# Order-of-work settings held for two first-pass steps instead of sixteen in a two-layer attention and GeGLU kernel

## The chip, the cores and the metric

The kernel runs on one core of one Trainium2 chip, in one launch. The metric is the device time of an execution in microseconds, as the median of several runs. TensorE (PE) does the matmuls and loads their weights (PEld), VectorE (DVE) and ScalarE (ACT) read its results out of the PSUM banks, GpSimd (POOL) works on SBUF alone, and SyncE (SP) issues the transfers.

## The reference

```python
def _A_ref(x, wqkv, wo):                 # S=2048, D=512, H=32 heads of Dh=16
    qkv = (x @ wqkv) ...                 # split into q, k, v by head
    scores = jnp.einsum("bhqd,bhkd->bhqk", q, k) * (Dh ** -0.5)
    p = _softmax(scores, axis=-1)
    o = jnp.einsum("bhqk,bhkd->bhqd", p, v)
    return o_reshaped @ wo
def _B_ref(x, w_gate, w_up, w_down):     # F=1792
    return (_gelu(x @ w_gate) * (x @ w_up)) @ w_down

x = A_x                                  # bfloat16, (1, 2048, 512)
x = x + _A_ref(_layernorm(x), A_wqkv, A_wo)
x = x + _B_ref(_layernorm(x), B_w_gate, B_w_up, B_w_down)
x = x + _A_ref(_layernorm(x), A_wqkv, A_wo)
x = x + _B_ref(_layernorm(x), B_w_gate, B_w_up, B_w_down)
```

Two layers with the same weights: attention over 2,048 tokens with 32 heads of 16 channels each, then a gated feed-forward part.

## The kernel before

All of `x`, the weights, K and V stay in SBUF. Queries are taken in blocks of 512 tokens (256 for the last two of the second layer, of which the last is split further at its end), and heads in 8 groups of four. One block and one group make a *unit*. A head has only 16 channels, so its scores use a 32-row strip of the PE array, and the four heads of a group lie on four strips.

**First pass.** For each unit, each 128 queries, each 512 keys and each head, one strip matmul (`p1_emit`, L1671) puts 128 x 512 scores into a PSUM bank, and DVE takes the maximum of each row, over one bank or two banks at once (L1686). A full unit has 64 such banks. `pos["p1"]` counts them in halves: two banks are one *first-pass step*, and the whole program has 2,048 steps. The maxima go through a few small POOL operations (L1027 to L1032) and a transfer (L1056) into an extra row of the queries, so that the second pass subtracts them inside its matmul. For some heads the maximum over two key blocks is *folded*: a matmul with the difference of the two blocks (`f_emit`, L1495), a relu on ACT (L1502) and a combined add and maximum on DVE (L1681).

**Second pass.** Strip matmuls with keys as rows (`p2_emit`, L1550) fill a bank with transposed scores, ACT takes the exponential of one bank or two (L1522), and `pv_emit` (L1575) multiplies them with V and a column of ones, using the whole array, into bank 7. When a unit is done, ACT copies bank 7 out (L1080) and POOL divides by the sum (L1086, L1091).

**The rest** runs in between as *chains* (Python generators that say what they wait for): projections and GEMMs in pieces (L782), their copies out of PSUM on ACT or DVE (L797, L799), the gate and the product of the feed-forward part (L1156 to L1238), layer norms, output projection, transfers. Each chain has a due time in first-pass steps.

**What sets the order.** Nothing is ordered by hand. While the program is being built, a loop (L1711 to L1864) keeps a clock for each engine, with a fixed length for each kind of instruction, and decides again and again what PE issues next: a bank for the first pass, one or two for the second, both, a piece of a chain, or a PV group. The other engines' instructions are put in behind the matmul that they read. Each engine then runs its own list in that order, with semaphores between the lists. Where the planner sees PE loaded below 0.55 (`WARM`) over its last 3.413 us, it adds a *filler* (`warm_emit`, L1704), a matmul of 240 columns whose result nobody reads.

The loop's decisions depend on 19 settings, and these are the subject here:

```python
STRETCH = 16
...
if pos["p1"] >= STRETCH * stretch[0]:
    if stretch[0] < len(PLAN):
        SPC, SPLIT, S1C, S2C, OV, LIM, NT, P2B, LAG, LAGT, FL, GL, FX, AHD, DUE, DUEM, PIECE, GP, NPV = PLAN[stretch[0]]
    stretch[0] += 1
```

`S1C` and `S2C` say how long before DVE or ACT runs dry its next bank is wanted, `SPC` and `SPLIT` how much may be lost by issuing both passes together, `OV` and `LIM` how far other work may run past that moment, `NT` and `P2B` how many and which banks the second pass may take at a time, `LAG`, `LAGT`, `FL`, `GL` and `FX` from which lead of the first pass on banks, copies and folding are given to the one or the other side, `AHD`, `DUE` and `DUEM` how far ahead due work is looked at, `PIECE` and `GP` in how many matmuls a GEMM is cut, and `NPV` when fillers are held to a higher load near the end of a unit. `PLAN` has 129 rows, one for each 16 steps.

Of the kernel before, what the change touches and what calls it, by code (L numbers as in the profile page):

```python
# [18 lines left out]
STRETCH = 16  # L20
PLAN = [
# [269 lines left out]
_T_MM = 1.0 / 2400.0  # L291
# [19 lines left out]
def _build(nc, x_in, wqkv, wo, wg, wu, wd, out, layer_blocks=((512, 512, 512, 512), (512, 512, 512, 256, 256)),  # L311
# [16 lines left out]
    with es:  # L328
# [62 lines left out]
        mode = ["full"]  # L391
        since = [0]
        T_DMA = 0.63
        act = []
        tw = {}
        tr = {}
        SEM = 0.06
# [1537 lines left out]
```

## Time and profile before

| | |
|---|---|
| time, median of 3 runs | 2483.9 us (2483.87 to 2483.9) |
| span of the profiled execution | 2482.0 us (no time of its own is given beside it; the median lies 1.9 us above) |
| instructions | 69,365 |
| PE busy | 2412.7 us, 97% |
| DVE busy | 2411.0 us, 97% |
| ACT busy | 2346.2 us, 95% |
| POOL busy | 1323.6 us, 53% |
| mean granted TensorE clock | 1.000 |

An engine counts as busy from an instruction's start to its end; the records of neighbours can overlap, so a busy engine may still have short gaps between starts. PE's busy time includes the fillers. In a group of instructions the first number is their busy time, the second the mean length of one in ns, the third the idle time of the engine just before them, followed by what ended most of it. "issue" stands for time in which the engine waited for nothing that the profile shows.

### The profile page before, as it was taken

The numbers are of one execution on the slowest core, as the hardware profiler recorded it, in microseconds if no ns is written. First come the engines' busy times: TensorE is split into PE (matmuls) and PEld (weight loads), VectorE is DVE, ScalarE is ACT, GpSimd is POOL, SyncE is SP. The second block draws the span as 40 slices with busy tenths as digits, with TensorE's granted clock in tenths as the row PEclk, the third lists the DMA queues.
The fourth block names the chain that finished last, engine by engine and source line by source line (L and its number), as shares of the span: only waits on it lengthen the run. The fifth ranks groups of instructions, "written<-read, shape, count | busy, mean of one in ns | idle before, by whom it ended". The sixth has DMA issues, their size and how long they took to land.

```text
span 2482.0 us, 69365 instructions
## 1 busy us (share of the span) xinstructions
PE 2412.7 (97%) x29824; PEld 1148.1 (46%) x29824; DVE 2411.0 (97%) x3167; ACT 2346.2 (95%) x3230; POOL 1323.6 (53%) x2182
## 2 busy tenths in 40 slices
PE   8999999999999999999999999999999999999999
PEld 3444444444444444444433555554444444544456
DVE  9999999999999999999999999999999999999995
ACT  7999999999999999999976999999999999999897
POOL 5121148965779367957143211379517882379472
PEclk9999999999999999999999999999999999999999
DMA  3110000000000000000000000000000000000000
GB/s 96 46 57 6 6 4 6 2 4 4 4 4 2 4 4 4 4 6 6 11 11 14 5 4 4 4 4 2 6 8 7 2 2 11 5 4 2 12 5 10
DMA packets 27387, 25.12 MB, mean 10 GB/s; under 512 B 9544, under 2 KB 26056, under 8 KB 27080
## 3 DMA queue, kind: packets, MB, share of 16 engines
q1 hardware_dynamic: 27080, 20.69, 2.9%
q8 instruction: 233, 3.82, 0.6%
q14 instruction: 74, 0.61, 0.1%
HBM read 9.70 MB, written 2.10 MB: 5 GB/s over the span
## 4 chain that ended last, share of the span: by engine, by line
PE 40%; DVE 37%; ACT 21%; issue 1%; POOL 1%; POOLq 0%; ACTq 0%; DVEq 0%
DVE PM L1686 35%; ACT SCR L1522 19%; PE PS L1671 13%; PE PS L782 10%; PE PS L1575 9%; PE PS L1550 4%; PE PS L1704 3%; DVE SCR L1681 1%; ACT SCR L1162 0%; ACT SCR L1502 0%; DVE HT L585 0%; PE PS L1495 0%; ACT AO L1236 0%; PE PS L904 0%; ACT XNT L799 0%
## 5 line engine op out<-in xcount | busy, mean ns | idle before, releaser
L1686 DVE TENSOR_REDUCE PM<-PS 128x1 f32<-128x512 f32 (+1 forms) x2586 | 2241.0, 932 | 33.1 <-PE PS L1550 11.6
L1522 ACT ACTIVATE SCR<-PS 128x1024 bf16<-128x1024 f32 (+1 forms) x2507 | 2029.0, 899 | 61.5 <-PE PS L1550 40.1
L1671 PE MATMUL PS<-KT,QT 32*128 32x512 bf16 x3940 | 1037.1, 384 | 38.6 <-DVE PM L1686 23.3
L1550 PE MATMUL PS<-QT,KT 32*128 32x512 bf16 (+2 forms) x4864 | 954.7, 349 | 6.8 <-ACT SCR L1522 5.2
L1575 PE MATMUL PS<-VP,SCR 128*128 128x51 bf16 (+1 forms) x16384 | 817.5, 187 | 12.0 <-ACT SCR L1522 6.9
L1575 PEld LDWEIGHTS PS<-VP,SCR 128*128 128x128 bf16 x16384 | 575.2, 96 | 509.0 <-issue 428.9
L1671 PEld LDWEIGHTS PS<-KT,QT 32*128 32x128 bf16 x3940 | 247.6, 91 | 515.7 <-DVE PM L1686 314.7
L1086 POOL TENSOR_TENSOR RL<-ACCS,CM 128x16 f32<-128x16 f32 (+2 forms) x66 | 179.6, 2722 | 384.8 <-ACT ACCS L1080 384.6
L1704 PE MATMUL PS<-WV,ZER 128*128 128x240 bf16 x1924 | 361.9, 265 | 1.2 <-ACT SCR L1522 1.1
L1550 PEld LDWEIGHTS PS<-QT,KT 32*128 32x128 bf16 x4864 | 241.6, 91 | 70.9 <-ACT SCR L1522 41.3
L1027 POOL TENSOR_TENSOR PM<-PM 128x32 f32<-128x32 f32 (+2 forms) x76 | 18.5, 243 | 305.1 <-DVE PM L1686 292.8
L1704 PEld LDWEIGHTS PS<-WV,ZER 128*128 128x128 bf16 x1924 | 147.9, 96 | 49.5 <-issue 39.6
L1238 POOL TENSOR_TENSOR HT<-HT,AO 128x512 bf16<-128x512 bf16 (+1 forms) x109 | 121.3, 1115 | 81.4 <-ACT AO L1236 80.4
L782 PE MATMUL PS<-XNT,WU 128*128 128x512 bf16 (+2 forms) x560 | 138.9, 339 | 1.2 <-ACT AO L1236 1.0
L782 PE MATMUL PS<-XNT,WG 128*128 128x512 bf16 (+2 forms) x560 | 139.7, 338 | 0.2 <-DVE XNT L797 0.2
L782 PE MATMUL PS<-WD,HT 128*128 128x512 bf16 x448 | 135.8, 381 | 0.2
L1275 POOL TENSOR_TENSOR KD<-KT 128x512 bf16<-128x512 bf16 x74 | 85.4, 1154 | 76.1 <-PE PS L1495 71.5
L1156 POOL TENSOR_TENSOR SCR<-HT 128x512 bf16<-128x512 bf16 (+1 forms) x98 | 96.0, 980 | 30.3 <-ACT HT L799 15.0
L1166 POOL TENSOR_TENSOR HT<-HT,SCR 128x512 bf16<-128x512 bf16 (+1 forms) x98 | 106.2, 1085 | 4.2
L1160 POOL TENSOR_TENSOR SCR<-SCR,HT 128x512 bf16<-128x512 bf16 (+1 forms) x98 | 106.3, 1086 | 1.8
L1681 DVE CUSTOM_DVE_ANT_0 SCR<-PS,SCR 128x512 bf16<-128x512 f32 x156 | 100.2, 686 | 1.9 <-PE PS L1495 0.6
L1106 POOL TENSOR_TENSOR X<-X,AO 128x512 f32<-128x512 f32 x42 | 53.2, 1268 | 84.4 <-ACT AO L1104 83.9
(129 smaller groups left out, 1560.4 us busy)
## 6 DMA issues: line engine op xcount, KB each, us to landing
KT<-SG SPq DMA_DIRECT2D x64, 64.0 KB
QT<-SG SPq DMA_DIRECT2D x56, 64.0 KB
QT<-MT SPq DMA_DIRECT2D x216, 1.0 KB
out_dram<-AO SPq DMA_DIRECT2D x16, 128.0 KB, 1.7
WG<-in_B_w_gate_dram SPq DMA_DIRECT2D x4, 448.0 KB, 4.3
WU<-in_B_w_up_dram SPq DMA_DIRECT2D x4, 448.0 KB, 4.8
WD<-in_B_w_down_dram SPq DMA_DIRECT2D x4, 384.0 KB, 4.5
QT<-MT SPq DMA_DIRECT2D x72, 0.5 KB
```

Source lines behind the costliest of these rows:

```text
L782: ins = e.matmul(out_ap, lhsT=l, rhs=r_, start=(i == 0), stop=(i == n - 1))
L1086: emit("pool", lambda e: e.tensor_tensor(RL[:, s, 0:4 * nq], lsum, CM1[:, 0:4 * nq], op=ALU.pow), r=[("ACCS", s), ("CM1",)], w=[("RL", s)] ...
L1160: emit("pool", lambda e: e.tensor_tensor(u, u, ht, op=ALU.mult), r=[ku, kh], w=[ku], dur=0.18 + n / 520.0)
L1166: emit("pool", lambda e: e.tensor_tensor(ht, ht, u, op=ALU.mult), r=[ku, kh], w=[kh], dur=0.18 + n / 520.0)
L1238: emit("pool", lambda e, ft=ft, o=o: e.tensor_tensor(HV[:, ft, :], HV[:, ft, :], AO[:, o, 0:n], op=ALU.mult), r=[("AO", o)] + ht_keys(ft, ...
L1522: emit("act", lambda e: e.activation(dst, src, ACTF.Exp, scale=DH ** -0.5), r=[BK[bk + i] for i in range(cnt)], w=[("PT", i) for i in slot ...
L1550: ins = e.matmul(bank(bk)[:, i * n:(i + 1) * n], lhsT=KT[32 * j:32 * j + 32, g, kt * 128:(kt + 1) * 128], rhs=QT[32 * j:32 * j + 32, s, c0 ...
L1575: ins = e.matmul(acc, lhsT=PT[:, slot, i * nh + (qt - q0) * 128:i * nh + (qt - q0 + 1) * 128], rhs=AP(VP, (kt * H + 4 * g + j) * 17, [[NTT ...
L1671: ins = e.matmul(bank(b), lhsT=QT[32 * j:32 * j + 32, s, qt * 128:(qt + 1) * 128], rhs=KT[32 * j:32 * j + 32, g, kb * 512:(kb + 1) * 512], ...
L1681: emit("dve", lambda e, i=i, b=b, sl=sl: e.tensor_tensor_reduce(PT[:, sl, :], bank(b), PT[:, sl, :], 1.0, -3.0e38, ALU.add, ALU.max, po[:, ...
L1686: emit("dve", lambda e: e.tensor_reduce(po, PS[:, bs[0]:bs[0] + cnt, :], axis=AX.X, op=ALU.max), r=bks, w=[("PM", sm) + h[1:] for h in hs] ...
L1704: return e.matmul(PS[:, b, NACC:512], lhsT=ZER[:, :], rhs=WV[:, 0, 0:512 - NACC], start=(b != 7), stop=(b != 7), skip_group_check=True)
```

## The change

`STRETCH` becomes 2, and `PLAN` becomes a dictionary: the settings that hold from step 2k on stand under the key k, and where a key is missing the last ones stay. It has 416 entries with 272 different sets of settings, among them all 104 different sets of before. Taken step by step, 657 of 1,025 pairs of steps have the settings that they had before. The list from which the planner reckons PE's load is kept as a queue with a running sum, which gives the same load. No function that emits an instruction is changed, and no buffer, size or bank count.

```diff
+import collections
...
-STRETCH = 16
-PLAN = [
-    (0.1, 0.15, 0.45, 0.42, 0.3, -0.05, 1, 1, 62, 84, 8, 60, 0.0, 2.0, 0, 2, 2, 2, 7),
-    (0.1, 0.15, 0.45, 0.42, 0.3, -0.05, 1, 1, 62, 84, 8, 60, 0.0, 2.0, 0, 2, 2, 2, 7),
-    (0.3, 0.3, 0.45, 0.42, 0.2, -0.05, 1, 1, 62, 84, 8, 20, 0.3, 1.5, 0, -14, 2, 2, 7),
...
+STRETCH = 2
+PLAN = {
+    0: (0.1, 0.15, 0.45, 0.42, 0.3, -0.05, 3, 1, 62, 84, 8, 60, 0.0, 2.0, 0, 2, 2, 2, 7),
+    2: (0.15, 0.5, 0.55, 0.42, 0.1, -0.05, 1, 2, 30, 124, 8, 100, 0.1, 2.0, 20, 6, 1, 2, 11),
+    6: (0.1, 0.0, 0.45, 0.62, 0.3, -0.05, 1, 1, 62, 84, 8, 60, 0.7, 2.0, 0, 2, 2, 2, 7),
+    7: (0.1, 0.15, 0.45, 0.42, 0.3, -0.05, 1, 1, 62, 84, 8, 60, 0.0, 2.0, 0, 2, 2, 2, 7),
...
-        act = []
+        act = collections.deque()
+        act_sum = [0.0]
+
+        def act_add(t, used):
+            act.append((t, used))
+            act_sum[0] += used
+
...
-                act.append((start, busy, n * (used or cols) * _T_MM))
+                act_add(start, n * (used or cols) * _T_MM)
...
-                    act.append((t, n * cols * _T_MM, n * cols * _T_MM / 4))
+                    act_add(t, n * cols * _T_MM / 4)
...
-                if stretch[0] < len(PLAN):
+                if stretch[0] in PLAN:
...
             while act and act[0][0] < now - 3.413:
-                act.pop(0)
-            load = sum(c for _, _, c in act) / 3.413
+                act_sum[0] -= act.popleft()[1]
+            load = act_sum[0] / 3.413
```

More of the change, by code (lines that the diff above doesn't have):

```diff
@@ L17 @@
 GELU_B = 0.044715
-STRETCH = 16
-PLAN = [
[129 rows of a table removed]
-]
+STRETCH = 2
+PLAN = {
[416 rows of a table added]
+}
 class _Op:
```

538 rows, old and new, of the table PLAN are left out of this document.

## The prediction

> **What bounds the kernel now.** I read the page first: the busy shares, the line of the granted clock, and the chain that ended last.
>
> ```profile
> span 2482.0 us, 69365 instructions
> PE 2412.7 (97%) x29824; PEld 1148.1 (46%) x29824; DVE 2411.0 (97%) x3167; ACT 2346.2 (95%) x3230; POOL 1323.6 (53%) x2182
> PEclk9999999999999999999999999999999999999999
> PE 40%; DVE 37%; ACT 21%; issue 1%; POOL 1%; POOLq 0%; ACTq 0%; DVEq 0%
> DVE PM L1686 35%; ACT SCR L1522 19%; PE PS L1671 13%; PE PS L782 10%; PE PS L1575 9%; PE PS L1550 4%; PE PS L1704 3%; DVE SCR L1681 1%; ACT SCR L1162 0%; ACT SCR L1502 0%; DVE HT L585 0%; PE PS L1495 0%; ACT AO L1236 0%; PE PS L904 0%; ACT XNT L799 0%
> ```
>
> Three engines are filled at once, and the chain goes from one to the other: row maxima on DVE (L1686), exponentials on ACT (L1522), matmuls on PE that feed both. There is no single wait to remove. What an order of work can change is the time between instructions. The same groups with their shapes kept apart give the prices, and the idle time before each:
>
> ```profile
> L1522 ACT ACTIVATE SCR<-PS 128x1024 bf16<-128x1024 f32 x1589 | 1560.3, 1065 | 48.8 <-PE PS L1550 32.5 <-PE PS L1671 0.2
> L1686 DVE TENSOR_REDUCE PM<-PS 128x2 f32<-128x1024 f32 x1198 | 1452.4, 1220 | 21.3 <-PE PS L1671 6.3 <-PE PS L1550 6.0
> L1686 DVE TENSOR_REDUCE PM<-PS 128x1 f32<-128x512 f32 x1388 | 932.2, 683 | 11.9 <-PE PS L1550 5.5 <-PE PS L1671 1.5
> L1522 ACT ACTIVATE SCR<-PS 128x512 bf16<-128x512 f32 x918 | 549.2, 613 | 12.6 <-PE PS L1550 7.7
> L1681 DVE CUSTOM_DVE_ANT_0 SCR<-PS,SCR 128x512 bf16<-128x512 f32 x156 | 100.2, 686 | 1.9 <-PE PS L1495 0.6 <-PE PS L1671 0.4 <-PE PS L1550 0.2
> L1502 ACT ACTIVATE SCR<-PS 128x1024 bf16<-128x1024 f32 x75 | 78.7, 1050 | 10.5 <-PE PS L1495 10.4
> L799 ACT ACTIVATE HT<-PS 128x512 bf16<-128x512 f32 x71 | 44.0, 620 | 0.0
> L1681 DVE DVE_READ_ACCUMULATOR2_ANT PM<- 128x1 f32 x156 | 13.1, 84 | 0.0
> L797 DVE CAST HT<-PS 128x512 bf16<-128x512 f32 x13 | 8.9, 682 | 0.1
> ```
>
> DVE stands still for 33.2 us (21.3 + 11.9) before all 2,586 row maxima together, ACT for 61.4 us (48.8 + 12.6) before all 2,507 exponentials. To see where, I asked for the busy time in forty stretches of 62 us:
>
> ```profile
> core 0: us, PE busy (x) PEld busy (x) DVE busy (x) ACT busy (x) POOL busy (x), PEclk, DMA share, GB/s
> 868.00:930.00 62.00, 60.07 (x760) 28.00 (x759) 61.96 (x71) 59.22 (x82) 39.94 (x87) 1.00 0.02 4
> 1302.00:1364.00 62.00, 60.44 (x464) 23.54 (x461) 57.82 (x105) 37.59 (x49) 19.23 (x51) 1.00 0.06 14
> 1488.00:1550.00 62.00, 60.14 (x869) 31.80 (x867) 61.19 (x74) 62.00 (x71) 10.82 (x12) 1.00 0.02 4
> 2418.00:2480.00 62.00, 60.02 (x950) 40.85 (x948) 33.48 (x74) 45.88 (x86) 18.93 (x43) 1.00 0.03 8
> ```
>
> Three kinds of stretch: DVE full (868 to 930, 61.96 of 62), ACT full (1488 to 1550, 62.00), and the end, where 28.5 us of DVE's 71.0 us of idle time (2482.0 less 2411.0) lie. At the turn between the layers (1302 to 1364) ACT is the one that starves. In the full stretches there is next to nothing visible to take. But the records of neighbouring instructions overlap, so "full" hides a little:
>
> ```profile
> 1411.59 29.45 ACT L1522 ACTIVATE SCR<-PS 128x1024 bf16<-128x1024 f32 x32
> ```
>
> Thirty-two exponentials in 29.45 us are 0.920 us each, where one record lasts 1.065 us. An exponential that starts 0.1 us late therefore still looks busy. The slack is somewhat more than the idle columns say, and still a few per cent at most.
>
> **What the change moves.** No source line of an instruction changes; what changes is the order that the planner writes, and with it the way in which some banks are evicted. I counted both built programs, instruction by instruction. Nothing on SP changes in number, so no transfer is added. On POOL there is one more two-column memset of PM, on an engine 53% busy. The last 1,449 PE instructions stand in the same order in both programs, and they hold the last 87 first-pass matmuls; after the last of these the four compute streams are the same too. So the 28.5 us at the end stay. Of PE's 29,824 instructions some 3,900 stand elsewhere, spread over nearly every stretch of the program in between; it is a small reshuffle.
>
> DVE: 6 one-bank maxima fewer (6 x 0.683 = 4.1 us), 1 two-bank maximum more (1.2 us), 2 folded maxima more with their reads (2 x (0.686 + 0.084) = 1.5 us), 1 copy of a gate tile fewer (0.7 us): 2.0 us less. ACT: 20 one-bank exponentials more (20 x 0.613 = 12.3 us), 10 two-bank ones fewer (10 x 1.065 = 10.7 us), 1 two-bank relu more (1.05 us), 1 gate copy more (0.6 us): 3.3 us more. So the work is as good as unchanged, and what counts is the waiting.
>
> The best sign of that is a count. The planner puts a filler matmul (L1704, output never used) where PE would else be less than 0.55 loaded (WARM) by its own reckoning. Two rows price it:
>
> ```profile
> L1704 PE MATMUL PS<-WV,ZER 128*128 128x240 bf16 x1924 | 361.9, 265 | 1.2 <-ACT SCR L1522 1.1
> 1345.68 0.89 PE L1704 MATMUL PS<-WV,ZER 128*128 128x240 bf16 x7
> ```
>
> Seven fillers in a row take 0.89 us, the last of them 0.265, so each other one occupies (0.89 - 0.265) / 6 = 0.104 us; the code counts 240 columns at 1/2400 us, 0.1 us. The changed program has 1,876 fillers, 48 fewer, and all other matmuls are the same in number. That is 4.8 us of PE time. Where fillers run, the load is held near 0.55, so a stretch with a given amount of real work needs fewer of them only if it is shorter, or if its real work lies more evenly. If it is all the former, the order is tighter by 4.8 / 0.55 = 8.7 us. If it is all the latter, by nothing. I take 8.7, because the counts fall in stretches that fillers fill as well as in others; zero stays in the range. The 2.0 us of DVE work are part of it and not added again.
>
> Two things are given back. The first is PE's change from strip matmuls (L1671, L1550, L1495) to full-array ones, which the table of waits prices:
>
> ```profile
> PEld PS L1575 <- issue: 428.9, 1875, 0.4
> PEld PS L1671 <- DVE PM L1686: 314.7, 1001, 1.6
> PEld PS L782 <- issue: 105.3, 462, 0.4
> ACT SCR L1522 <- PE PS L1550: 40.1, 119, 3.9
> PEld PS L1704 <- issue: 39.6, 174, 0.4
> DVE PM L1686 <- PE PS L1550: 11.6, 40, 0.8
> ```
>
> 428.9 / 1,875 = 0.229 us each, and L782 and L1704 have the same price (0.228). The changed order has 22 more such changes into L1575, 9 fewer into L782 and 10 fewer into L1704: 3 more, 0.7 us. The second is ACT's 3.3 us, of which 21%, ACT's share of the chain, is taken as lying on the path: 0.7 us. The rest is covered by ACT's own 135.8 us of idle time (2482.0 less 2346.2); in stretches like 1488 to 1550 that cover does not exist, and the whole 3.3 us would count.
>
> Sum: -8.7 + 0.7 + 0.7 = -7.3 us. On the profiled span that is 2482.0 - 7.3 = 2474.7 us; the median of the runs lies 1.9 us above that span (2483.9), and the runs agree within 0.03 us, so the forecast is 2476.6 us. What is late next is DVE itself: 314.7 us of weight loads wait for a maximum to free its bank, and a tighter order only lets PE wait longer there.
>
> One rule of the skill speaks against fewer fillers. The profile has a granted clock of 1.00 in each of the four stretches above and full marks in all forty slices, with fillers 1.3 us apart on average (2482.0 / 1,924). The Trainium skill, "TensorE: Matmul & The Clock Gate", Part 1, says that a matmul engine left idle for a window of about 3.4 us is set back to half its clock. By that rule 48 fillers fewer are harmless unless they leave a hole of that length; no run here shows a hole.
>
> **The rivals.** First, *the settings fit the planner's clock and not the chip* (0.20). The planner reckons with one fixed length for each kind of instruction and with no scatter. L1671 and L1550 take turns at the same banks, and the waits of DVE and ACT on L1550 are short and many (40 of 0.29 us, 119 of 0.34 us): these are what an order tuned to 0.1 us must hit. If the saved 8.7 us come back as some 30 such waits (30 x 0.3 = 9 us), nothing is left: 2484, give or take 5. For it speaks that only one instruction in eight moves; against it, that the tight row of ACT shows a plan carried out without gaps for 29 us.
>
> Second, *slower: the new changes of PE's mode lie where DVE is the bound* (0.14). The 22 further changes into L1575 cost 22 x 0.229 = 5.0 us if each delays a maximum, while the 19 saved ones lie before GEMMs and fillers that nobody waits for; with ACT's 3.3 us in full it makes +8.3 and up to 2492.2, less whatever part of the 8.7 is real. It decides once DVE's idle time before L1686 grows by more than 5 us from 33.2, with L1575 up in PE's waits. Against it: PE's 97% contains fillers, so it can give way.
>
> Third, *the clock falls* (0.04). If a stretch with load 0.55 is granted less than 0.55 of the clock, PE becomes its bound; at 0.5 a 62 us slice takes 0.55 / 0.5 = 1.1 times as long, +6.2 us, and one such slice gives 2490. That is the rule of the page named above, carried through. Nothing in the trace points to it.
>
> Fourth, *more gain than the fillers tell* (0.10). In stretches without fillers the count is blind. If half of the idle time of DVE before its maxima goes (16.6 us), it is 2467.
>
> That the change does nothing at all is excluded by the counts; that it does nothing to the time is the first rival.
>
> **How the numbers follow.** The forecast has 0.52, its own range 2472 to 2481. A measurement of this kernel can tell about 0.2%, 5 us, from no change: the borders are 2478.9 and 2488.9. Of the forecast's chance 0.08 lies above 2478.9. Faster: 0.44 + 0.10 = 0.54. Same: 0.08 + 0.20 = 0.28. Slower: 0.14 + 0.04 = 0.18. The range 2466 to 2490 leaves out about half of the fourth rival below and most of the second and third above, some 0.2.
>
> **What would show it.** Right: DVE's and ACT's busy times within 4 us of 2411 and 2346, filler busy time down by 2 to 3%, the last 62 us unchanged, and the saving spread in pieces of 0.1 to 0.5 us per stretch of 62 us, as less idle time before L1686 and L1522 or as closer starts behind the same busy share. Wrong: idle time before L1686 above 38 us; a granted clock under 1.00; or a saving that sits in one place, such as the turn of the layers.

## The result and the profile after

The changed kernel takes 2473.9 us (median of 5 runs, 2473.87 to 2474.03), the kernel before 2483.9 us (2483.87 to 2483.9): 10.0 us less, a ratio of 0.9959 with a 95% interval of 0.9947 to 0.9971. The forecast was 2476.6 us with a range of 2466 to 2490.

In the profile after, all line numbers are 294 higher (L1686 is L1980, L1522 is L1816, L1550 is L1844, L1575 is L1869, L1704 is L1998), except around the planner's load. First the span, the busy times and the chain that ended last:

```profile
span 2472.2 us, 69280 instructions
PE 2407.5 (97%) x29776; PEld 1147.3 (46%) x29776; DVE 2404.8 (97%) x3165; ACT 2343.1 (95%) x3242; POOL 1320.7 (53%) x2183
PEclk9999999999999999999999999999999999999999
PE 39%; DVE 38%; ACT 22%; issue 1%; POOL 1%; POOLq 0%; DVEq 0%; ACTq 0%
```

The picture is the same as before, 9.8 us shorter: DVE's busy time is down by 6.2 us and its idle time by 3.6 (71.0 to 67.4). No engine's share of the chain moves by more than one point. The groups with their shapes kept apart (busy us, mean ns of one, idle us before):

```profile
L1816 ACT ACTIVATE SCR<-PS 128x1024 bf16<-128x1024 f32 x1579 | 1550.3, 1071 | 41.4 <-PE PS L1844 27.9 <-PE PS L1965 0.4
L1980 DVE TENSOR_REDUCE PM<-PS 128x2 f32<-128x1024 f32 x1199 | 1451.2, 1217 | 21.3 <-PE PS L1844 6.4 <-PE PS L1965 6.4 <-PE PS L1789 0.3
L1980 DVE TENSOR_REDUCE PM<-PS 128x1 f32<-128x512 f32 x1382 | 925.2, 681 | 9.0 <-PE PS L1844 3.4 <-PE PS L1965 2.1
L1816 ACT ACTIVATE SCR<-PS 128x512 bf16<-128x512 f32 x938 | 559.8, 613 | 12.8 <-PE PS L1844 8.9
L1998 PE MATMUL PS<-WV,ZER 128*128 128x240 bf16 x1876 | 353.7, 265 | 0.8 <-ACT SCR L1816 0.7
```

The idle time before the maxima went from 33.2 to 30.3 us, before the exponentials from 61.4 to 54.2. The table of waits names the same waits, each a little shorter than before but the first, the weight loads of L1575 (L1869 here), which wait 3.2 us more:

```profile
PEld PS L1869 <- issue: 432.1, 1888, 0.4
PEld PS L1965 <- DVE PM L1980: 302.3, 977, 1.1
PEld PS L1076 <- issue: 104.4, 459, 0.4
PEld PS L1998 <- issue: 37.5, 163, 0.4
ACT SCR L1816 <- PE PS L1844: 36.8, 112, 3.9
DVE PM L1980 <- PE PS L1844: 9.8, 37, 0.7
```

And the end is untouched. The last 52 us of the kernel before, then the last 52 us after (busy time by engine: PE, PEld, DVE, ACT, POOL):

```profile
2430.00:2482.00 52.00, 48.79 (x743) 33.77 (x742) 21.70 (x58) 33.92 (x69) 8.99 (x20) 1.00 0.04 12
```

```profile
2420.20:2472.20 52.00, 48.73 (x743) 33.71 (x741) 21.63 (x58) 33.84 (x69) 8.90 (x20) 1.00 0.04 12
```

### The profile page after: what moved, and what is told of

Read it like the earlier page. It is cut to its first block, busy times and chain, and to the rows that moved or that the text cites. A ratio compares the mean times of both kernels' runs of the same rounds, so it can differ in the third digit from the quotient of the medians.

```text
span 2472.2 us, 69280 instructions
## 1 busy us (share of the span) xinstructions
PE 2407.5 (97%) x29776; PEld 1147.3 (46%) x29776; DVE 2404.8 (97%) x3165; ACT 2343.1 (95%) x3242; POOL 1320.7 (53%) x2183
## 4 chain that ended last, share of the span: by engine, by line
PE 39%; DVE 38%; ACT 22%; issue 1%; POOL 1%; POOLq 0%; DVEq 0%; ACTq 0%
DVE PM L1980 36%; ACT SCR L1816 20%; PE PS L1965 13%; PE PS L1076 10%; PE PS L1869 9%; PE PS L1844 4%; PE PS L1998 3%; DVE SCR L1975 1%; DVE HT L879 0%; ACT SCR L1456 0%; PE PS L1789 0%; ACT SCR L1796 0%; ACT AO L1530 0%; PE PS L1198 0%; ACT ACCS L1374 0%
## 5 line engine op out<-in xcount | busy, mean ns | idle before, releaser
L1980 DVE TENSOR_REDUCE PM<-PS 128x1 f32<-128x512 f32 (+1 forms) x2581 | 2234.2, 930 | 30.3 <-PE PS L1844 9.8
L1816 ACT ACTIVATE SCR<-PS 128x1024 bf16<-128x1024 f32 (+1 forms) x2517 | 2028.6, 900 | 54.3 <-PE PS L1844 36.8
L1844 PE MATMUL PS<-QT,KT 32*128 32x512 bf16 (+2 forms) x4864 | 951.7, 349 | 6.3 <-ACT SCR L1816 4.6
L1869 PE MATMUL PS<-VP,SCR 128*128 128x51 bf16 (+1 forms) x16384 | 818.6, 187 | 11.6 <-ACT SCR L1816 6.9
L1869 PEld LDWEIGHTS PS<-VP,SCR 128*128 128x128 bf16 x16384 | 576.5, 96 | 510.4 <-issue 432.1
L1965 PEld LDWEIGHTS PS<-KT,QT 32*128 32x128 bf16 x3938 | 247.5, 91 | 505.4 <-DVE PM L1980 302.3
L1998 PE MATMUL PS<-WV,ZER 128*128 128x240 bf16 x1876 | 353.7, 265 | 0.8 <-ACT SCR L1816 0.7
L1844 PEld LDWEIGHTS PS<-QT,KT 32*128 32x128 bf16 x4864 | 241.2, 91 | 72.4 <-ACT SCR L1816 44.1
L1998 PEld LDWEIGHTS PS<-WV,ZER 128*128 128x128 bf16 x1876 | 143.4, 96 | 46.5 <-issue 37.5
L1450 POOL TENSOR_TENSOR SCR<-HT 128x512 bf16<-128x512 bf16 (+1 forms) x98 | 95.9, 979 | 29.9 <-ACT HT L1093 14.7
```

The source lines that it names most:

```text
L1816: emit("act", lambda e: e.activation(dst, src, ACTF.Exp, scale=DH ** -0.5), r=[BK[bk + i] for i in range(cnt)], w=[("PT", i) for i in slot ...
L1844: ins = e.matmul(bank(bk)[:, i * n:(i + 1) * n], lhsT=KT[32 * j:32 * j + 32, g, kt * 128:(kt + 1) * 128], rhs=QT[32 * j:32 * j + 32, s, c0 ...
L1869: ins = e.matmul(acc, lhsT=PT[:, slot, i * nh + (qt - q0) * 128:i * nh + (qt - q0 + 1) * 128], rhs=AP(VP, (kt * H + 4 * g + j) * 17, [[NTT ...
L1965: ins = e.matmul(bank(b), lhsT=QT[32 * j:32 * j + 32, s, qt * 128:(qt + 1) * 128], rhs=KT[32 * j:32 * j + 32, g, kb * 512:(kb + 1) * 512], ...
L1980: emit("dve", lambda e: e.tensor_reduce(po, PS[:, bs[0]:bs[0] + cnt, :], axis=AX.X, op=ALU.max), r=bks, w=[("PM", sm) + h[1:] for h in hs] ...
L1998: return e.matmul(PS[:, b, NACC:512], lhsT=ZER[:, :], rhs=WV[:, 0, 0:512 - NACC], start=(b != 7), stop=(b != 7), skip_group_check=True)
```

## Experiments: where the gain sits, and what the settings are

Four theories were put to the test. **O**: the order is tighter throughout, and the fewer fillers are the shadow of that. **F**: the PE time of the fillers itself is the gain. **P**: the gain sits in one place. **D**: it is DVE's 2.0 us of work less.

**One layer at a time.** The first kernel takes the new settings for the first layer's 1,024 steps and the old ones after it, the second the other way round.

```diff
# e1: new settings for keys under 512, the old ones from there on; e2: the reverse
-PLAN = {all 416 entries}
+PLAN = {the new entries of one layer, the old rows of the other, each under its key}
```

> New settings for the first layer's 1,024 steps, old ones for the second; 25 fillers fewer than the kernel before, no other matmul more or less. Theory O (a tighter order throughout, which the filler count shadows at 0.1/0.55 = 0.18 us each): 4.5 us less than before, 2479.4. Rival P (the saving sits in one layer, or at its turn or end): nothing (2483.9) or all of it (2473.9).

> Old settings for the first layer, new ones for the second; 22 fillers fewer than before, no exponentials in more one-bank pieces. Theory O: 4.0 us less, 2479.9, so that both halves make up the whole. Rival P: all or nothing. Rival D (the saving is DVE's 2.0 us of work less): DVE has 6 one-bank maxima and one copy fewer and 3 two-bank maxima more here, 4.8 less 3.7 = 1.1 us, so 2482.8.

Measured: 2479.0 and 2479.0 us (ratios 0.9979 to the kernel before, 0.997 to 0.9989 each), 5.1 us less each, where the kernel before took 2484.1 beside them. The halves make up the whole (10.2 against 10.0), so P falls, and so does D: the second kernel has 1.1 us less DVE work and gains 5.1. The traces show why the halves can be put together. From 1194 us to the end the first kernel issues its last 15,751 PE instructions in the order of the kernel before, and from 1199 us on the second one issues its last 15,729 in the order of the new kernel. At the turn of the layers the program comes back to the same order, whichever settings ran until then. In pieces, 25 fillers fewer went with 5.1 us, 22 with 5.1, 48 with 10.0: 0.20 to 0.23 us each, somewhat more than the 0.18 of the forecast.

**The same settings, two steps late; and one entry less.**

```diff
# e3: every key but 0 one higher
-    2: (0.15, 0.5, 0.55, 0.42, 0.1, -0.05, 1, 2, 30, 124, ...),
+    3: (0.15, 0.5, 0.55, 0.42, 0.1, -0.05, 1, 2, 30, 124, ...),
...
# e4: the entry with key 272 (step 544) left out, all others as they are
```

> The new settings, all 416 of them in the same sequence, each two first-pass steps later. 456 fillers more than the new kernel, 280 mode changes of PE more, 92 more one-bank exponentials and 46 fewer two-bank ones. If the settings are rules that suit a phase of the work, two steps out of 2,048 change next to nothing: 2474 to 2476. If they are a record of choices that fit one exact state of the queues: by the fillers 456 x 0.18 = 83 us more, 2557. Both planner and chip must agree for that; if the fillers' number tells little about time (they only fill holes), well under that, some 20 us.

> One of the 416 entries is left out (the one for step 544), so the settings of the entry before it stay for one entry longer; all others are the same. 306 fillers more than the new kernel. Theory O with settings that fit one exact state: 306 x 0.18 = 56 us more, 2530, lost between step 544 and the turn of the layers at step 1,024. Rival (settings as rules of a phase): under 1 us.

Measured: 2607.9 us (ratio to the kernel before 1.05, 1.0484 to 1.0515) and 2557.3 us (1.0293, 1.0276 to 1.031), 134 and 83 us slower than the new kernel. The settings are not rules for a phase of the work. They are a record of choices, each made for the state of the queues that the choices before it had left. With all of them two steps late the program loses thirteen times what the whole record gained, and with one setting kept for 16 steps too long (steps 544 to 559, where the old table has the same setting as the new one) eight times. The fillers' count told the direction and again too little of the size: 456 and 306 more, 0.29 and 0.27 us each.

How the loss of e4 lies was a surprise. Busy time in stretches of 20 us around the turn of the layers, first in the new kernel, then with the one entry left out (after the stretch and its length come PE, PEld, DVE, ACT and POOL):

```profile
1180.00:1200.00 20.00, 19.28 (x282) 10.29 (x281) 19.95 (x26) 19.84 (x23) 5.16 (x10) 1.00 0.01 2
1200.00:1220.00 20.00, 19.10 (x281) 10.08 (x277) 19.47 (x27) 20.00 (x23) 0.00 (x0) 1.00 0.01 2
1220.00:1240.00 20.00, 19.61 (x164) 7.76 (x163) 19.84 (x33) 15.41 (x24) 9.23 (x12) 1.00 0.11 28
```

```profile
1180.00:1200.00 20.00, 19.26 (x256) 9.55 (x257) 17.90 (x23) 19.42 (x24) 17.31 (x38) 1.00 0.01 2
1200.00:1220.00 20.00, 18.49 (x213) 9.98 (x211) 0.42 (x1) 16.17 (x22) 16.95 (x44) 1.00 0.01 2
1220.00:1240.00 20.00, 19.19 (x169) 8.58 (x167) 11.51 (x25) 12.72 (x19) 1.56 (x7) 1.00 0.03 7
```

DVE starts one instruction in the 20 us from 1200 on. The timeline of e4 says what it waits for, on DVE and, in the lines after the gap, on POOL. Line numbers are 293 above those of the kernel before here: L1090 is the copy out of PSUM (L797), L1197 the transposes (L904), L1156 to L1187 the layer norm on POOL (L863 to L894), L1379 the softmax division (L1086).

```profile
1197.72 0.42 DVE L1090 COPY XNT<-PS 128x512 bf16<-128x512 bf16 x1
1207.61 0.42 DVE L1090 COPY XNT<-PS 128x512 bf16<-128x512 bf16 x1 [9.47 <-PE PS L1197]
1222.57 0.42 DVE L1090 COPY XNT<-PS 128x512 bf16<-128x512 bf16 x1 [14.53 <-PE PS L1197]
...
1205.97 0.77 POOL L1187 TENSOR_SCALAR XN<-X,LNS 128x512 bf16<-128x512 f32 x1
1206.75 0.61 POOL L1156 TENSOR_TENSOR SC<-X 128x256 f32<-128x256 f32 x1
1217.13 2.92 POOL L1379 TENSOR_TENSOR RL<-ACCS,CM 128x16 f32<-128x16 f32 x1
1220.73 0.77 POOL L1187 TENSOR_SCALAR XN<-X,LNS 128x512 bf16<-128x512 f32 x1
```

DVE's copies of transposed tiles wait for PE's transposes, and these for layer norms that POOL computes one token tile after the other. The last of them runs from 1206.75 to 1221.50 us, with a softmax division pushed in between. Until they are through, the second layer has no keys for its first pass. In the new kernel POOL has finished them before 1200 us and stands idle.

**The layer norm moved.** If that is the cause, it must help to take these layer norms elsewhere, in the kernel with the entry left out:

```diff
-            yield from ln_to_xnt(tts, ("in", la), lambda tt: not la or ffn_rec.get(tt) == la - 1, due)
+            yield from ln_to_xnt(tts, ("in", la), lambda tt: not la or ffn_rec.get(tt) == la - 1, due, la > 0 and tts[0] == 4)
```

> The kernel with the one entry left out (2557.3 us), in which the layer norm of four token tiles (tokens 512 to 1,023, second layer) is taken on DVE instead of POOL. Theory H (the lost time is not spread, but stands in a few holes where late layer norms on POOL keep the second layer's keys back): DVE's holes of 9.5 and 14.5 us at the turn go, 24 us, and what follows from them, at a cost of four times two DVE passes of 0.69 us, 5.5 us: 2538 or less, and far less if the loss at the end (32 us) was a consequence too. Rival S (the loss is made of many small waits, because the settings no longer fit): the holes move elsewhere, 2550 to 2563.

Measured: 2502.4 us (ratio to the kernel before 1.0074, 1.0057 to 1.0091), 54.9 us less, for four token tiles on DVE. In the same 20 us DVE now stands idle for 6.4 us instead of 19.6:

```profile
1200.00:1220.00 20.00, 18.35 (x226) 9.54 (x224) 13.63 (x24) 16.79 (x20) 4.13 (x9) 1.00 0.04 9
```

How much of the 54.9 us is the hole itself can be read from the traces. Each kernel loads the same 16,384 weights for the second pass (L1575 in the kernel before). The time at which the same one of them is loaded tells how far a kernel lies behind the new one:

| us behind the new kernel, which is at | 1164 us | 1347 us | 1526 us | 2449 us, the last load |
|---|---|---|---|---|
| e4, one entry left out | 15.9 | 43.5 | 45.5 | 85.7 |
| e9, layer norm moved as well | 17.8 | 25.3 | 28.3 | 28.3 |

At the turn (1164 to 1347 us) e4 loses 27.6 us and e9 7.5. So the hole is worth some 20 us, and Theory H holds for it. The larger part lies behind it. From 1536 us on e9 issues its last 12,372 PE instructions in the order of the new kernel, and it loses nothing more. e4 comes back to that order for good only with its last 18 instructions, and loses another 40 us on the way. One late chain on POOL, which is 51% busy, thus cost some 20 us by itself, and the order that was missed after it cost more. That the one follows from the other is argued only: why e9 comes back to the order and e4 does not was not tested. The 16 to 18 us before the turn are lost in both.

## Experiments: what the fillers do

The next kernels leave fillers out of the finished lists, or issue them twice; the planner still reckons with one each, so every other instruction keeps its place.

```diff
         def warm_emit(b):
...
+            n_warm[0] += 1
+            op = sch.op
+            if n_warm[0] % 40 == 0:          # e5, on the kernel before; 2 in e6, all in e7, 8 in e10, 4 in e11
+                sch.op = lambda *a, **k: None
             emit_pe(fn, 1, 512 - NACC, r=[("ZER",), ("WV",)], w=[BK[b]])
+            sch.op = op
```

> The kernel before with every fortieth filler left out (48 of 1,924), all else in its old order. Theory O (the fillers' number is the shadow of the saving): within 0.5 us of 2483.9. Rival F (the saving is the PE time of the 48 fillers themselves): 4.8 to 8.7 us less, 2475 to 2479.

Measured: 2483.5 us where the kernel before took 2483.9 (ratio 0.9999, 0.9989 to 1.0008), 0.4 us for 48 fillers, within the noise of no change. F falls: the fillers' own time was hidden, and their number only tells how long the rest takes.

```diff
         def warm_emit(b):                    # e8, on the new kernel
             def fn(e):
-                return e.matmul(...)
+                for _ in range(2):
+                    ins = e.matmul(...)
+                return ins
```

> The new kernel with each filler issued twice (1,876 more, 188 us of PE time more). Theory O, with fillers in holes of 0.1 to 0.2 us on PE: part of the second filler sticks out and delays the next bank; from nothing to 188 us, estimate 30 us (one in six of them), 2504. Rival F: each filler lies on the path, 2474 + 188 = 2662.

Measured: 2589.8 us (ratio to the kernel before 1.0426, 1.0409 to 1.0444), 115.9 us more than the new kernel for 188 us of PE time, 62% of it; the expectation of one in six was far off. The chain goes over to PE:

```profile
PE 69%; DVE 20%; ACT 8%; issue 1%; DMA 0%; SPq 0%; POOL 0%; POOLq 0%; ACTq 0%; DVEq 0%
```

One filler in its place costs next to nothing, a second behind it costs 0.062 us on average: the planner has used up most of PE's gaps.

> The new kernel with every second filler left out (938 fewer), order otherwise the same. If fillers only hold the clock up and the clock is granted in windows, PE's load falls from 0.55 to about 0.5 in the filled stretches; rival C (the clock falls) shows as a granted clock under 1.00 and a longer time, by tens of us. If there is margin: granted clock 1.00 and the same 2473.9 or a few us less, since 938 x 0.1 = 94 us of PE time is freed.

> The new kernel without any filler (1,876 fewer). Rival C: granted clock well under 1.00 in the stretches that had most fillers, 2500 or more. If fillers do nothing: 2460 to 2474, with PE's time before DVE's banks freed.

> The new kernel with every eighth filler left out (234 fewer, 23 us of PE time). If fillers in the places that the planner gave them are covered, as the 48 of the kernel before were (0.4 us for 4.8 us of PE time), the time falls by 0.4 / 48 x 234 = 2.0 us, 2471.9, with a granted clock of 1.00 in all runs. If the clock already needs them: runs between 2473 and 2480 that differ from each other by several us, as with half of the fillers.

> The new kernel with every fourth filler left out (469 fewer, 47 us of PE time). By the same count 3.9 us less, 2470.0, if the granted clock stays at 1.00; if its margin ends between a quarter and a half of the fillers, runs spread over some us with the lowest near 2472.

| fillers left | time, us | runs, us | granted clock of the runs |
|---|---|---|---|
| all 1,876 | 2473.9 | 2473.87 to 2474.03 | 0.999 to 1.000 |
| seven in eight | 2472.2 | 2472.1 to 2473.4 | 0.999 to 1.000 |
| three in four | 2473.3 | 2471.0 to 2475.6 | 0.997 to 1.000 |
| half | 2484.2 | 2472.7 to 2500.3 | 0.977 to 0.997 |
| none | 2693.6 | 2691.1 to 2701.7 | 0.774 to 0.778 |

Rival C holds without fillers, and with half of them to a degree that differs from run to run. Seven in eight came out as priced (2471.9 us expected). Three in four did not reach the 2470.0 us expected at the full clock.

Without fillers the granted clock comes down in most slices, while PE looks as busy as before; the line of the page, and two of its stretches (the clock is third from the end):

```profile
PEclk8855556997659696998589575589886798589978
310.00:372.00 62.00, 60.74 (x577) 25.18 (x576) 53.03 (x73) 52.58 (x58) 9.94 (x16) 0.50 0.02 4
1364.00:1426.00 62.00, 59.94 (x313) 19.38 (x317) 59.65 (x105) 43.31 (x65) 27.56 (x50) 0.99 0.06 15
```

The fillers thus earn 219.7 us by the clock. With half of them the time depends on the run and follows the granted clock: of ten runs the fastest took 2472.7 us at 0.997, the slowest 2500.3 at 0.977. The Trainium skill, "TensorE: Matmul & The Clock Gate", Part 1, describes a free-running window of about 3.4 us and two clocks, full and half, and warns that one kernel differs from run to run with the phase of that window. The traces agree with the window and the two clocks: without fillers the granted clock is 1.00 or 0.50 and nothing else, and each of the 52 stretches between two of its changes is a whole number of windows of 3.413 us. The rule of an idle gap of 3.4 us, as the prediction cites it, does not explain the falls: the longest time without a matmul record in this run is 1.58 us, and PE was busy in 60.74 of 62 us at a clock of 0.50. What came before a fall is a low load. Counted as the planner counts it (1/2400 us for a column, a quarter of that in a strip matmul), the window before each of the 30 falls in the profiled runs with none, half or three in four of the fillers has a load of 0.16 to 0.40, an estimate from the records; the planner fills up to 0.55. Some windows as low as 0.33 kept the full clock, so no sharp threshold comes out.

The kernel with seven in eight fillers has the lowest median, with a ratio of 0.9954 (0.9939 to 0.9969) to the kernel before. Its runs (2472.1 to 2473.4 us) lie below all of the changed kernel's (2473.9 to 2474.0), by 1.75 us in the median. The two did not run side by side; the kernel before took 2483.9 us beside each.

## Why the prediction was right, and where it was off

**What bounds it.** Right: no single wait went, no engine took over, and the end kept its length to 0.1 us of DVE's busy time. The 10 us came in two equal parts from the two layers. By the weight loads of the second pass the new kernel leads by 2.6 us when the kernel before is at 637 us, by 4.9 at 1352, 5.4 at 1718 and 9.9 at 2386. The saving is spread, but not in even pieces: from 1352 to 1718 us, where ACT is full nearly throughout, it grows by 0.5 us only. Of the named signs, the filler time (2.3% less), ACT's busy time and the end came as forecast; DVE's busy time moved by 6.2 us and not by 4 at most.

**The fillers as a measure.** The largest term, -8.7 us, was taken in full although zero was possible; the whole gain was 10.0. That a shorter program needs fewer fillers held in sum (e1 and e2), and that the fillers' own time is not the saving was shown (e5). But the term was too small: a filler fewer went with 0.20 to 0.23 us instead of 0.18. Place by place the count says little. At 204 us the new kernel leads by 1.3 us with three fillers more, and from 934 to 1096 us 15 fillers fewer go with 1.4 us. That the sum came so close is in part luck. The fourth rival's stretches that hold no fillers and get shorter unseen would explain the missing part; that was not tested by itself.

**What is given back.** PE's changes of mode: forecast 0.7 us, and the three rows of "issue" waits went from 573.8 to 574.0 us, 0.2 more. ACT's pieces: forecast 3.3 us more busy time, with 0.7 on the path. ACT's busy time fell by 3.1 us instead (2346.2 to 2343.1). The term was wrong in sign: it priced each piece at the mean length of a record and left out the overlap. ACT's records added up grew by 14.7 us (2704.6 to 2719.3), but they overlap by 17.7 us more. With 0.5 us too much for the one and 0.7 for the other, 1.5 of the 2.7 us between forecast and result are left for the fillers' term.

**DVE's work.** By the count of pieces 2.0 us less busy time, measured 6.2. For the other 4.2 us the prediction had named closer starts behind the same busy share. On DVE more overlap is not what the records show: added up they exceed the busy time by 221.4 us before and by 218.8 after. The records themselves got shorter, from 1220 to 1217 ns and from 683 to 681. But with the old order they measured 1216 and 680 in e5, at 2410.2 us busy, so a shorter record is no mark of the new order. Where the 4.2 us come from stays open.

**What is late next.** Wrong. PE was to wait longer for DVE's banks; it waited less, 302.3 instead of 314.7 us. Why is argued only: a matmul and its maximum make a cycle, and what shortens the waits of the one may shorten those of the other.

**The rivals.** That the settings fit the planner's clock and not the chip is refuted for the path as it stands (short waits went down, 40 to 37 and 119 to 112), though each fits only the order that it was chosen in. New changes of mode on the path: the idle time before the maxima fell. The clock: full marks in all slices with 48 fillers fewer; with 469 fewer than that it was 0.997 to 1.000 (e11). More gain than the fillers tell was partly true.

## What to carry to other kernels

Where a planner leaves fillers in what it takes for idle time, their number is a cheap reading of how long the rest takes, too low rather than too high here. A table of settings chosen step by step holds for the order in which it was chosen. An edit that changes the order can cost more than the table gained, and much of the loss may sit far behind the edit, as here from a chain of an idle-looking engine on that is no longer in time. Where the program comes back to the old order the settings hold again, as they did here at the turn of the layers in e1 and e2 and from 1536 us on in e9, so a long table may be tested in pieces between such places. Price an extra instruction by what happens when it is doubled, not by what happens when it is removed: here 0.062 us for a filler more against 0.008 for a filler less.

## What the runs showed of the hardware

The granted TensorE clock was 1.00 or 0.50, changed only after whole windows of 3.413 us, and fell to 0.50 although PE was busy 98% of a 62 us stretch by its records and never without a matmul for more than 1.58 us. Leaving out fillers that make up 188 us of 2,474 cost 219.7 us. With an eighth of them gone the clock held (0.999 to 1.000), with half of them the same program took from 2472.7 to 2500.3 us.
